# A fused attention and two-layer MLP kernel: where the word between three integer steps lies (SBUF or PSUM)

## The chip, the cores and the metric

The kernel runs on one core of a Trainium2 chip. The metric is the device time of one execution in microseconds (us), the median of three runs. Engine names in profile rows: PE is TensorE's matmuls, PEld its weight loads, DVE is VectorE, ACT is ScalarE, POOL is GpSimd, SP is SyncE (which issues the DMAs here).

## The reference

Masked attention over 4 batches, 8 heads, 576 positions and 64 values per head (heads 0 to 3 see the last 32 positions, heads 4 to 7 every 32nd one), then two layers of an MLP on 2304 tokens of width 512, each with a hidden width of 2048:

```
attn = softmax(mask(q @ k.T / 8)) @ v            # float32
x = attn as (2304, 512)
h = maximum(x @ w_in, 0);  x = (h * h) @ w_out               # first layer
h = x @ w_in2;  g = P(h) / Q(h);  out = g @ w_out2           # second layer
```

P is a cubic and Q a quadratic polynomial in h (Q with absolute values). The weights of both layers reach the kernel as 64-bit floats, which it turns into 32-bit ones itself.

## The kernel before, in words

**Work.** Tokens lie in 6 blocks j of 384. For a block and each of 16 hidden slices f, an "h unit" (line 406, 12 matmuls) gives h[j, f] in a PSUM bank, `act1` (lines 411 to 421) squares its positive part and splits it into a rounded part gh and a remainder gl, and an "acc unit" (line 433, 12 matmuls) adds gh and gl times the second weights into four PSUM banks. In block 0 `act1` works in place: relu (L411), square (L412) and the rounding cast to gh (L420) on ScalarE, the subtraction to gl (L421) on VectorE. The second layer does the same with P/Q in place of the square.

**Weights.** Slice f of the first layer comes in two parts (part 0 for h, part 1 for acc), so there are 32 conversions, called here the 1st to the 32nd, in the order 0_0, 1_0, 2_0, 0_1, 3_0, 1_1, 4_0, 2_1, 5_0, 3_1, ... 15_0, 13_1, 14_1, 15_1 (slice_part). Each is: a DMA of the raw 64-bit words (`load_w`, L185, 512 KB, ring `wraw` of 3 buffers), then `to_f32`: one ScalarE activation (L195) writes a scaled absolute value into a word of the ring `w32` (3 buffers), and three VectorE integer steps (L196, L197, L198) finish the word; L197 and L198 also read the raw words. Then `split_w` makes the rounded weights wh (GpSimd L214, every fourth time ScalarE L212) and the remainder wl (GpSimd L215, the first four on VectorE). The DMA of conversion n+3 waits for L198 of conversion n.

**Attention.** 48 groups of a head pair go through slots: scores (L271 mask, L279), maximum (L290), exponential (L303), normalization (L311, L312, L314), transposes (L321), values (L337), output (L362, L363). Groups 0 to about 11 come first; the next run between the units of block 0.

**PSUM.** All PSUM tiles (ps_s, ps_t, ps_v, h, the four acc) are taken from one pool of 8 banks under one tag (`bufs=8`). A tile that takes a bank waits until the tile that had it is done with.

**Order.** A list scheduler in the framework orders each engine's instructions from the program's order, dependences and free buffers; at run time each engine takes its own list strictly in order. In the first layer the order of the conversions among other work is the scheduler's. The second layer's conversions (the same `to_f32`, with layer 1) run during blocks 1 to 4 and go back to DRAM.

Of the kernel before, what the change touches and what calls it, by code (L numbers as in the profile page):

```python
# [11 lines left out]
I32 = mybir.dt.int32  # L12
BF16 = mybir.dt.bfloat16
AF = mybir.ActivationFunctionType
ALU = mybir.AluOpType
# [3 lines left out]
P = 128  # L19
# [3 lines left out]
DM, DFF = 512, 2048  # L23
# [133 lines left out]
def moe_kernel(ctx, tc, qk, vp, w1, w2, a, b, masks, eye, out):  # L157
    nc = tc.nc
# [14 lines left out]
    psum = ctx.enter_context(tc.tile_pool(name="psum", bufs=8, space=PSUM))  # L173
# [14 lines left out]
    def to_f32(layer, f, part, raw):  # L188

        lo, hi = raw[:, :, 0], raw[:, :, 1]
        w = stage.tile([P, DM], I32, tag="w32", bufs=3, name=f"w32_{layer}_{f}_{part}")
        wf = w.bitcast(F32)
        nc.scalar.activation(wf, hi.bitcast(F32), AF.Abs, scale=2.0**-112)  # L195
        nc.vector.tensor_scalar(w, w, 3, 0x7FFFFFFF, ALU.logical_shift_left, ALU.bitwise_and)  # L196
        nc.vector.scalar_tensor_tensor(w, hi, -0x80000000, w, ALU.bitwise_and, ALU.bitwise_or)  # L197
        nc.vector.scalar_tensor_tensor(w, lo, 29, w, ALU.logical_shift_right, ALU.bitwise_or)  # L198
        return wf

    def w_place(layer, f):
# [263 lines left out]
    def feed_w(n):  # L465
        for _ in range(n):
            if wq:
                f, part = wq.pop(0)
                c = slice(part * DM, (part + 1) * DM)
                wh, wl = wt[0, f] if part else w_place(0, f)  # L470
                split_w(wh[:, c], wl[:, c], to_f32(0, f, part, load_w(0, f, part)))
# [14 lines left out]
    def spill_w(f, part):  # L486

        wf = to_f32(1, f, part, load_w(1, f, part))
        parts = [stage.tile([P, DM], F32R, tag="w32", bufs=3, name=f"sp{c}{f}_{part}") for c in "hl"]
        split_w(*parts, wf)  # L490
        for z, t in enumerate(parts):
            nc.sync.dma_start(w2_dram[z, f][:, part * DM : (part + 1) * DM], t.bitcast(F32))
# [97 lines left out]
    for j, f in steps:  # L590
# [10 lines left out]
        ps = psum.tile([P, 512], F32, tag="ps", name=f"h0_{j}_{f}")  # L601
# [46 lines left out]
```

## Time and profile before

| | |
|---|---|
| time of three runs | 951.86 us median (951.51 to 952.64) |
| the profiled execution | 951.99 us, of which the span of the profile is 950.2 us |
| busy, share of the span | PE 95%, DVE 73%, POOL 64%, ACT 58% |
| 60 to 95 us | PE 28.0 of 35 us, DVE 33.4, POOL 27.6 |
| 95 to 130 us | PE 27.6 of 35 us, DVE 32.8, POOL 28.2 |
| 165 to 240 us | PE 74.4 of 75 us, DVE 40.9 |
| 570 to 950 us | PE 375.6 of 380 us, DVE 373.4 |

The span is the time between the first and the last recorded instruction. Busy times of engines overlap. PEclk in the rows is the share of TensorE's full clock that was granted. A wait of an engine is put down to the instruction that released it.

### The profile page before, as it was taken

The page shows a single profiled execution, that of the slowest core. Times are in us where ns is not written, and L with a number is a line of the kernel's source. Part 1 is how long each engine was busy: PE and PEld are TensorE (multiplying, and loading weights), DVE is VectorE, ACT ScalarE, POOL GpSimd, SP SyncE. Part 2 cuts the span into 40 slices and gives each one's busy share as a digit, 9 for nine tenths or more (in the row PEclk, how much of TensorE's full clock was granted, in tenths as well). Part 3 has the DMA queues.
Part 4 walks back from the last instruction along what each step waited for, and adds up shares of the span by engine and source line. Part 5 has one row for each costly group of instructions (what it writes and reads, how often), then busy time and mean ns, then how long its engine had stood idle before and what let it go on. Part 6 is the DMA issues. An engine that isn't in the chain of part 4 may idle for free.

```text
span 950.2 us, 14600 instructions
## 1 busy us (share of the span) xinstructions
PE 903.5 (95%) x5232; PEld 830.8 (87%) x5232; DVE 691.4 (73%) x792; ACT 548.8 (58%) x1391; POOL 609.6 (64%) x643
## 2 busy tenths in 40 slices
PE   7787689999999999999999999999999999999998
PEld 4576679999899989999999999999999899899896
DVE  3789993554545555544411579999999999999997
ACT  4765454453544445433323667676777777777774
POOL 3667772545545545534423468888888888888885
PEclk9798888999999999999999999999999999999999
DMA  8256451543533463434158550010010010000000
GB/s 306 82 177 206 142 184 67 180 159 121 191 128 107 147 196 101 133 133 134 67 203 285 187 175 18 9 51 9 9 50 9 9 51 10 15 28 1 34 1 34
DMA packets 40104, 98.55 MB, mean 104 GB/s; under 512 B 4704, under 2 KB 11616, under 8 KB 40032
## 3 DMA queue, kind: packets, MB, share of 16 engines
q1 hardware_dynamic: 40032, 97.62, 31.0%
q8 instruction: 41, 0.67, 0.3%
q14 instruction: 31, 0.25, 0.1%
HBM read 71.39 MB, written 26.21 MB: 103 GB/s over the span
## 4 chain that ended last, share of the span: by engine, by line
DVE 46%; PE 39%; POOL 5%; ACT 4%; issue 3%; DMA 2%; SPq 0%; POOLq 0%; ACTq 0%; DVEq 0%
DVE rq L530 23%; PE h L406 19%; PE acc L433 16%; DVE p L532 9%; DVE rq L541 7%; DVE w L197 2%; DVE w L198 2%; POOL wl L215 1%; PE ps_t L321 1%; DVE w L196 1%; PE ps_s L279 1%; PE ps_v L337 1%; DMA qk<-in_qk 1%; POOL wh L214 1%; DMA x_scratch<-x 1%
## 5 line engine op out<-in xcount | busy, mean ns | idle before, releaser
L406 PE MATMUL h<-xh,wh 128*128 128x384 f32 x768 | 259.5, 338 | 0.6 <-ACT p L527 0.5
L406 PE MATMUL h<-xh,wl 128*128 128x384 f32 x768 | 258.3, 336 | 0.0
L406 PE MATMUL h<-xl,wh 128*128 128x384 f32 x768 | 257.8, 336 | 0.0
L530 DVE RECIPROCAL rq<-w 128x384 f32<-128x384 f32 x96 | 243.9, 2541 | 17.2 <-POOL w L528 17.2
L406 PEld LDWEIGHTS h<-xh,wh 128*128 128x128 f32 x768 | 144.8, 189 | 6.8 <-ACT p L527 1.9
L406 PEld LDWEIGHTS h<-xl,wh 128*128 128x128 f32 x768 | 144.8, 188 | 3.8
L421 POOL TENSOR_TENSOR gl<-r,gh 128x384 fp32r<-128x384 f32 x75 | 75.8, 1011 | 110.2 <-ACT gh L420 96.1
L406 PEld LDWEIGHTS h<-xh,wl 128*128 128x128 f32 x768 | 144.5, 188 | 0.0
L549 POOL TENSOR_TENSOR gl<-rq,gh 128x384 fp32r<-128x384 f32 x96 | 115.1, 1199 | 39.8 <-ACT gh L548 39.8
L433 PE MATMUL acc<-gh,wh 128*128 128x384 f32 x384 | 132.6, 346 | 2.0 <-ACT gh L420 2.0
L433 PE MATMUL acc<-gl,wh 128*128 128x384 f32 x384 | 132.1, 344 | 2.0 <-DVE gl L421 2.0
L417 DVE TENSOR_TENSOR r<-r 128x384 f32<-128x384 f32 x75 | 57.1, 761 | 103.6 <-ACT r L416 103.3
L433 PE MATMUL acc<-gh,wl 128*128 128x384 f32 x384 | 131.4, 342 | 0.0
L528 POOL TENSOR_TENSOR w<-w,sq 128x384 f32<-128x384 f32 x96 | 97.4, 1014 | 46.6 <-ACT sq L525 46.6
L529 POOL TENSOR_TENSOR p<-p,hs 128x384 f32<-128x384 f32 x96 | 114.6, 1194 | 0.0
L563 PE MATMUL acc<-wh,gl 128*128 128x512 f32 x288 | 114.1, 396 | 0.2 <-POOL gl L549 0.2
L563 PE MATMUL acc<-wl,gh 128*128 128x512 f32 x288 | 113.7, 395 | 0.0
L563 PE MATMUL acc<-wh,gh 128*128 128x512 f32 x288 | 112.0, 389 | 0.0
L548 ACT CAST gh<-rq 128x384 fp32r<-128x384 f32 x96 | 49.4, 514 | 105.9 <-DVE rq L541 105.9
L532 DVE SCALAR_TENSOR_TENSOR p<-p,co,hs 128x384 f32<-128x384 f32 x96 | 99.2, 1033 | 0.0
L416 ACT ACTIVATE r<-h 128x384 f32<-128x384 f32 x75 | 36.7, 490 | 87.9 <-PE h L406 83.6
L420 ACT CAST gh<-r 128x384 fp32r<-128x384 f32 x75 | 38.5, 514 | 72.0 <-DVE r L417 71.8
(71 smaller groups left out, 1627.2 us busy)
## 6 DMA issues: line engine op xcount, KB each, us to landing
wraw<-in_w SPq DMA_DIRECT2D x64, 512.0 KB, 4.2
w_scratch<-sph SPq DMA_DIRECT2D x32, 256.0 KB, 4.1
w_scratch<-spl SPq DMA_DIRECT2D x32, 256.0 KB, 3.3
wh<-w_scratch SPq DMA_DIRECT2D x16, 512.0 KB, 3.7
wl<-w_scratch SPq DMA_DIRECT2D x16, 512.0 KB, 4.8
v<-in_vp SPq DMA_DIRECT2D x24, 256.0 KB, 4.6
qk<-in_qk SPq DMA_DIRECT2D x12, 416.0 KB, 5.0
x_scratch<-x SPq DMA_DIRECT2D x24, 192.0 KB, 2.6
```

The source lines that it names most:

```text
L406: nc.tensor.matmul(ps[:, :TB], w[:, c], x[:, kk, :], start=(kk == 0 and i == 0), stop=(kk == KT - 1 and i == 2))
L417: nc.vector.tensor_tensor(h, h, h, ALU.mult)
L421: (nc.vector if psum_h else nc.gpsimd).tensor_tensor(gl, h, gh.bitcast(F32), ALU.subtract)
L433: nc.tensor.matmul(acc[j][e][:, :TB], w[:, c], g, start=(f == 0 and i == 0), stop=(f == NF - 1 and i == 2))
L528: keep(nc.gpsimd.tensor_tensor(w, w, sq, ALU.add))
L529: keep(nc.gpsimd.tensor_tensor(p1, p1, hs, ALU.mult))
L530: keep(nc.vector.reciprocal(rq, w))
L532: keep(nc.vector.scalar_tensor_tensor(p1, p1, a1, hs, ALU.add, ALU.mult))
L541: keep(nc.vector.scalar_tensor_tensor(rq, p1, a0, rq, ALU.add, ALU.mult))
L548: keep(nc.scalar.copy(gh, rq))
L549: keep(nc.gpsimd.tensor_tensor(gl, rq, gh.bitcast(F32), ALU.subtract))
L563: nc.tensor.matmul(p, g[:, t * P : (t + 1) * P], w[:, c], start=(f == 0 and i == 0), stop=(f == NF - 1 and i == 2))
```

## The change

In the first layer alone, the word that goes from the first to the second and from the second to the third integer step is a new tile `bits` of the PSUM pool, in place of the `w32` word itself. The third step writes its result to the `w32` word as before. Nothing is added or taken away: each conversion still has one activation and three VectorE steps of 128x512 words.

```
         nc.scalar.activation(wf, hi.bitcast(F32), AF.Abs, scale=2.0**-112)
-        nc.vector.tensor_scalar(w, w, 3, 0x7FFFFFFF, ALU.logical_shift_left, ALU.bitwise_and)
-        nc.vector.scalar_tensor_tensor(w, hi, -0x80000000, w, ALU.bitwise_and, ALU.bitwise_or)
-        nc.vector.scalar_tensor_tensor(w, lo, 29, w, ALU.logical_shift_right, ALU.bitwise_or)
+        bits = w
+        if layer == 0:
+            bits = psum.tile([P, DM], I32, tag="ps", name=f"bits{f}_{part}")
+        nc.vector.tensor_scalar(bits, w, 3, 0x7FFFFFFF, ALU.logical_shift_left, ALU.bitwise_and)
+        nc.vector.scalar_tensor_tensor(bits, hi, -0x80000000, bits, ALU.bitwise_and, ALU.bitwise_or)
+        nc.vector.scalar_tensor_tensor(w, lo, 29, bits, ALU.logical_shift_right, ALU.bitwise_or)
         return wf
```

The 32 new tiles take their turn in the 8 banks, and the scheduler orders all five engines' lists anew, from the attention slots ahead of block 0 to its h unit 13. Behind that point the lists are the same. (Lines from 196 on move by 3 in the changed file: its integer steps are L199, L200 and L201, its h units L409, its acc units L436.) Three places:

On VectorE, at the last two conversions (14_1 and 15_1), the list before reads:

```order
L421 TENSOR_TENSOR gl_0_12_1469<-h_0_12_1453,gh_0_12_1468 128x384 [waits PE_49,Activation_49]
L198 SCALAR_TENSOR_TENSOR w_0_14_1_1247<-wraw_14_1_1245,w_0_14_1_1247 128x512 [waits DVE_49]
L196 TENSOR_SCALAR w_0_15_1_1256<-w_0_15_1_1256 128x512 [waits Activation_49]
L197 SCALAR_TENSOR_TENSOR w_0_15_1_1256<-wraw_15_1_1254,w_0_15_1_1256 128x512 [waits DMAHW3_49,DVE_49]
L290 TENSOR_REDUCE sm_0_2_1496<-ps_s_0_2_1484 96x4 [waits PE_49]
L198 SCALAR_TENSOR_TENSOR w_0_15_1_1256<-wraw_15_1_1254,w_0_15_1_1256 128x512 [waits DVE_49]
```

and the list of the change:

```order
L424 TENSOR_TENSOR gl_0_7_1250<-h_0_7_1234,gh_0_7_1249 128x384 [waits Activation_49]
L201 SCALAR_TENSOR_TENSOR w_0_13_1_1267<-wraw_13_1_1265,bits_1_1269 128x512 [waits DVE_49,Pool_49]
L199 TENSOR_SCALAR bits_1_1279<-w_0_14_1_1277 128x512 [waits Activation_49]
L200 SCALAR_TENSOR_TENSOR bits_1_1279<-wraw_14_1_1275,bits_1_1279 128x512 [waits DMAHW0_49,DVE_49]
L201 SCALAR_TENSOR_TENSOR w_0_14_1_1277<-wraw_14_1_1275,bits_1_1279 128x512 [waits DVE_49,Pool_49]
L199 TENSOR_SCALAR bits_1_1289<-w_0_15_1_1287 128x512 [waits Activation_49]
L200 SCALAR_TENSOR_TENSOR bits_1_1289<-wraw_15_1_1285,bits_1_1289 128x512 [waits DMAHW1_49,DVE_49]
L201 SCALAR_TENSOR_TENSOR w_0_15_1_1287<-wraw_15_1_1285,bits_1_1289 128x512 [waits DVE_49,Pool_49]
L424 TENSOR_TENSOR gl_0_8_1311<-h_0_8_1295,gh_0_8_1310 128x384 [waits PE_49,Activation_49]
L424 TENSOR_TENSOR gl_0_9_1342<-h_0_9_1326,gh_0_9_1341 128x384 [waits PE_49,Activation_49]
```

Before, the remainders gl of 13 units (0 to 12) stand ahead of the last conversion's third step; now those of 8 units do, and units 8 and 9 come behind it.

On TensorE, at the scores of groups 0_1 and 1_1 (behind h unit 9 in both), the list before has these rows:

```order
L271 MATMUL ps_s_0_1_1325<-cst 96x512
L271 LDWEIGHTS cst
L271 MATMUL ps_s_1_1_1326<-cst 96x512
L279 MATMUL ps_s_0_1_1325<-qk_0_1_837 96x128 [waits DMAHW2_49]
...
L321 MATMUL ps_t_0_0_1343<-ident,e_0_0_1075 128x96 [waits DVE_49]
```

and the list of the change:

```order
L274 LDWEIGHTS cst [waits DVE_49]
L274 MATMUL ps_s_0_1_1357<-cst 96x512 [waits PE_49]
L274 LDWEIGHTS cst
L274 MATMUL ps_s_1_1_1358<-cst 96x512 [waits DVE_49]
L282 MATMUL ps_s_0_1_1357<-qk_0_1_851 96x128 [waits DMAHW7_49]
...
L324 MATMUL ps_t_0_0_1375<-ident,e_0_0_1098 128x96 [waits DVE_49,Pool_49]
```

The tiles of these scores now take the banks of the words of conversions 14_1 and 15_1, and their first matmuls wait for VectorE; ps_t of group 0_0 takes the bank of h unit 9 and waits for gl of unit 9.

On ScalarE, at unit f = 2 of block 0, the list before reads:

```order
L411 ACTIVATE h_0_2_769<-h_0_2_769 128x384 [waits PE_49]
L420 CAST gh_0_1_736<-h_0_1_721 128x384 [waits Activation_49]
L412 ACTIVATE h_0_2_769<-h_0_2_769 128x384 [waits Activation_49]
L420 CAST gh_0_2_784<-h_0_2_769 128x384 [waits Activation_49]
L212 CAST wh_2_464<-w_0_2_1_664 128x512 [waits DVE_49]
```

and the list of the change:

```order
L195 ACTIVATE w_0_8_0_884<-wraw_8_0_882 128x512 [waits DMAHW4_49,Pool_49]
L414 ACTIVATE h_0_2_783<-h_0_2_783 128x384 [waits PE_49]
L415 ACTIVATE h_0_2_783<-h_0_2_783 128x384 [waits Activation_49]
L195 ACTIVATE w_0_6_1_894<-wraw_6_1_892 128x512 [waits DMAHW5_49,DVE_49,Pool_49]
L423 CAST gh_0_2_798<-h_0_2_783 128x384 [waits Activation_49]
```

The cast to gh of unit 2 stood ahead of the activation of conversion 5_0 (the 9th); now it stands behind that of 6_1 (the 16th), which waits for its raw words.

## Rows read from the trace of the kernel before

**Rows 1.** The page: busy time of the engines, and the chain that ended last.
```profile
PE 903.5 (95%) x5232; PEld 830.8 (87%) x5232; DVE 691.4 (73%) x792; ACT 548.8 (58%) x1391; POOL 609.6 (64%) x643
...
DVE 46%; PE 39%; POOL 5%; ACT 4%; issue 3%; DMA 2%; SPq 0%; POOLq 0%; ACTq 0%; DVEq 0%
```

**Rows 2.** Windows: stretch, length, busy PE, PEld, DVE, ACT, POOL, clock, DMA, GB/s.
```profile
60.00:95.00 35.00, 28.03 (x175) 25.18 (x176) 33.40 (x51) 19.20 (x59) 27.61 (x29) 0.90 0.65 208
95.00:130.00 35.00, 27.63 (x160) 25.64 (x159) 32.80 (x44) 17.75 (x48) 28.15 (x28) 0.85 0.51 171
...
165.00:240.00 75.00, 74.43 (x518) 70.83 (x517) 40.89 (x69) 35.73 (x110) 39.05 (x49) 1.00 0.49 156
```

**Rows 3.** Timeline of VectorE, 60 to 150 us: start, duration, instruction, [idle before].
```profile
61.82 0.68 DVE L198 SCALAR_TENSOR_TENSOR w<-wraw,w 128x512 int32<-128x512 int32 x1
...
96.81 0.17 DVE L312 RECIPROCAL sm<-sm 96x4 f32<-96x4 f32 x1 [2.46 <-POOL sm L311]
...
113.49 0.41 DVE L196 TENSOR_SCALAR w<-w 128x512 int32<-128x512 int32 x1
113.82 0.55 DVE L421 TENSOR_TENSOR gl<-h,gh 128x384 fp32r<-128x384 f32 x1
114.29 0.68 DVE L197 SCALAR_TENSOR_TENSOR w<-wraw,w 128x512 int32<-128x512 int32 x1
115.00 1.65 DVE L198 SCALAR_TENSOR_TENSOR w<-wraw,w 128x512 int32<-128x512 int32 x1
...
133.88 0.69 DVE L198 SCALAR_TENSOR_TENSOR w<-wraw,w 128x512 int32<-128x512 int32 x1
...
142.60 1.14 DVE L198 SCALAR_TENSOR_TENSOR w<-wraw,w 128x512 int32<-128x512 int32 x1
```

**Rows 4.** Windows of lines 196, 197, 198 alone: length, busy VectorE (count), clock.
```profile
48.00:149.00 101.00, 19.86 (x27) 0.87 0.56 181
...
48.00:149.00 101.00, 24.70 (x28) 0.87 0.56 181
...
48.00:149.00 101.00, 34.36 (x28) 0.87 0.56 181
```

**Rows 5.** Groups by line and shape, 0 to 240 us: busy, mean ns, idle before.
```profile
L417 DVE TENSOR_TENSOR r<-r 128x384 f32<-128x384 f32 x16 | 12.6, 787 | 13.3 <-ACT r L416 13.3
...
L290 DVE TENSOR_REDUCE sm<-ps_s 96x4 f32<-96x512 f32 x16 | 10.7, 677 | 0.0
...
L421 DVE TENSOR_TENSOR gl<-h,gh 128x384 fp32r<-128x384 f32 x16 | 8.8, 549 | 8.9 <-ACT gh L420 8.8
...
L288 DVE TENSOR_TENSOR ps_s<-ps_s,cst 96x512 f32<-96x512 f32 x4 | 2.6, 688 | 1.8 <-PE ps_s L279 1.8
```

**Rows 6.** DMA issues, 60 to 130 us: count, KB each, median us to landing.
```profile
wraw<-in_w SPq DMA_DIRECT2D x20, 512.0 KB, 3.9
```

**Rows 7.** Timeline of ScalarE, around 51 and 106 to 117 us.
```profile
51.52 1.30 ACT L195 ACTIVATE w<-wraw 128x512 f32<-128x512 f32 x2
...
106.47 0.48 ACT L420 CAST gh<-h 128x384 fp32r<-128x384 f32 x1
...
116.69 0.62 ACT L212 CAST wh<-w 128x512 fp32r<-128x512 f32 x1 [1.24 <-DVE w L198]
```

**Rows 8.** The chain of waits from 145 us: start, duration, what.
```profile
147.01 3.49 PE h L406 x12
...
159.17 2.08 PE h L406 x12
161.25 2.08 PE acc L433 x12
```

**Rows 9.** Timeline of TensorE: scores at 107, values and transposes at 135 to 139 us.
```profile
107.72 0.60 PE L271 MATMUL ps_s<-cst 96*96 96x512 bf16 x2
108.25 1.12 PE L279 MATMUL ps_s<-qk 64*96 64x128 f32 x16
...
135.43 0.55 PE L337 MATMUL ps_v<-at,v 128*64 128x96 f32 x8 [0.40 <-DVE gl L421]
...
139.19 0.52 PE L321 MATMUL ps_t<-ident,e 96*128 96x96 f32 x4 [3.21 <-POOL wh L214]
```

## The prediction

> **What bounds the kernel now.** The page comes first: TensorE is busy 95% of the span, yet VectorE holds 46% of the chain that ended last and TensorE 39% [rows 1]. Both can only be true if different stretches have different limits, so the windows come next [rows 2]. [...] From 165 to 240 us TensorE works 74.43 of 75 us. So first-layer conversions are VectorE's stretch, and what is gained or lost there passes to the end one for one: behind it TensorE is dense, and its instructions there are the same in both kernels.
>
> Then the conversions themselves. The 8th ends at 61.82 + 0.68 = 62.50 us, the 32nd at 142.60 + 1.14 = 143.74 us [rows 3]: 81.24 us for 24, or 3.39 each. One step is not one price: the third step took 0.69 us at 133.88 and 1.65 us at 115.00 [rows 3]. Grouped by line, the three steps cost 19.86, 24.70 and 34.36 us between 48 and 149 us, for 27, 28 and 28 instructions [rows 4]: 78.9 us, 2.82 per conversion. The reason to look for is in the neighbours: a subtraction of 128x384 with both inputs in SBUF (L417) took 787 ns, the one with one input in PSUM (L421) 549 ns [rows 5], while GpSimd was busy about 28 of 35 us throughout [rows 2].
>
> **The change part by part.** *The steps.* The trace has no integer step on PSUM. Bounds: an elementwise operation from and to PSUM, 512 wide, took 688 ns, a reduce of 512 from PSUM 677 ns, L421 549 ns for 384, which is 0.73 for 512 by width [rows 5]. Below, the first step could keep its present 0.41 [rows 3] and the others 0.68; above, nothing is shortened and each keeps today's means, 0.74, 0.88 and 1.23 [rows 4]. I take 0.69 for each, by the L288 row, which is nearest: 2.07 per conversion. Then 28 conversions cost 58.0 in place of 78.9 us, 21 us less of VectorE's time (the first step alone gets dearer, by 0.28 on an undisturbed one). There are no new instructions and no new DMAs.
>
> The rows show no dearer price for PSUM: 688 and 677 ns there, 0.68 and 0.69 us for undisturbed steps in SBUF [rows 3, 5]. [...]
>
> *Can the conversions use it?* A ring of three raw words feeds them: landing 3.9 us [rows 6], the activation 1.30 / 2 = 0.65 [rows 7], three steps 2.07, handoffs 0.2 (chosen), together 6.82 for three conversions, 2.27 each. VectorE's own pace is 2.07 plus 8 subtractions gl of 0.55 over 24 conversions, 2.25. So about 2.3 us per conversion is what both allow, against 3.39 now. If all was as before and nothing else waited, 24 x 1.09 = 26 us would be free, more than TensorE could use: it was idle only about 7 of each 35 us [rows 2].
>
> *The order.* The banks change more than the steps. The new words take turns with scores, transposes, values, h and acc, and the scheduler puts conversions far ahead: only units 0 to 7 have their gl before the last conversion ends, before it was 0 to 12. TensorE's work is no less; more of it lies behind the last conversion. What that costs is counted from the end of the 32nd conversion to the start of h unit 13.
>
> Before: 147.01 - 143.74 = 3.27 us [rows 3, 8], and unit 13 itself ran at the low clock, 3.49 in place of 2.08 us [rows 8], another 1.41. Together 4.68.
>
> Now: ScalarE first casts wh (0.62 [rows 7]) and does five operations of units 8 and 9 of 0.48 each [rows 7], VectorE the gl of 0.55 [rows 5], handoffs 0.2, together 3.8, before the transposes of group 0_0 can go on, since they take the bank that this gl releases. Then TensorE has three h units (3 x 2.08 = 6.24), acc 8, 9, 10 and 7 of the 12 matmuls of acc 11 (3.58 x 2.08 = 7.45) [rows 8], one pair of scores (from 107.72 to 109.37, 1.65), three value products (0.55 for two, 0.83) and four transposes (4 x 0.52 = 2.1) [rows 9]. That is 18.2, with the 3.8 before it 22.0. The work is the same that was done earlier; before, it lay beside conversions in TensorE's idle time.
>
> So the break-even is a 32nd conversion that ends at 143.74 + 4.68 - 22.0 = 126.4 us. By the pace alone it ends well ahead of that; the question is how many waits come on top.
>
> *When does the 32nd end?* The 8th: four of the first eight lie in the stretch of [rows 4], 4 x 0.75 = 3.0 us less; and the activation at 51.52 [rows 7], which the new order puts ahead of attention work, gives 2 more (an estimate): 57.5. Then 24 x 2.3 = 55.2. Attention on VectorE between them: four reduces (two of 0.68, two on fewer scores, taken at half), four reciprocals of 0.17 and eight narrow subtractions taken at the same 0.17 [rows 3, 5]: 4.1. Then the waits that the new order makes:
> - gl of unit 2 follows the 14th conversion, but its cast gh now stands on ScalarE behind the activation of the 16th, whose DMA starts only when the 13th is done. 3.9 + 0.65 + 0.48 + 0.2 after the 13th, 2.3 of it covered by the 14th: 2.9 us in which the conversions queued behind it wait.
> - Reciprocals stand close behind their reduces. One such wait for GpSimd was 2.46 [rows 3]; taken once more, 2.5.
> - Three conversions whose activation stands behind another unit's three ScalarE operations (3 x 0.48): 4.2.
> - h units 3 and 5 whose acc follows directly leave TensorE idle, and the next unit then runs at the low clock, 1.4 us more each by [rows 8]: 2.8.
>
> That is 12.4, and the end 57.5 + 55.2 + 4.1 + 12.4 = 129.2 us, 2.8 behind the break-even. The profiled execution lasted 951.99 us, 0.13 above the median of 951.86, which lies on its span of 950.2 with 1.8 outside. 951.99 + 2.8 = 954.8.
>
> **The rivals.** *Faster: the waits are short.* The same chain, with the other sign. If the DMAs run ahead (landing 3.9 is a median) and the reciprocals' waits lie under other steps, only 5 or 6 us of the 12.4 remain, the 32nd ends near 122.8, and h unit 13 starts 3.6 us earlier: 948.4. For it: 21 us off the engine that is the bound is much, and only 2.8 us in 129 lie between the two; against it: VectorE's list is strictly in order, and each of its new waits holds all conversions. It decides when the end falls below 126.4.
>
> *No change.* Gain and tail cancel to within 1.9 us, an end between 124.5 and 128.3: about 952.
>
> *The low clock.* TensorE had 0.85 to 0.90 in this stretch [rows 2] and goes through a unit in 3.49 at the low clock. If, with acc waiting behind each h, the clock falls for six units in place of two, 4 x 1.41 = 5.6 us are added: about 960.
>
> *The change does not do what it says.* The steps stay as long as today, because GpSimd is not what stretches them or because the raw word in SBUF is enough for it. Then 24 conversions take 24 x 2.82 = 67.7 in place of 55.2, and the tail stays: about 967.
>
> **How the numbers follow.** The forecast of a late 32nd conversion with a long tail has 0.48; its own range, with 0.1 us either way per conversion, is 952.4 to 957.2. The short waits have 0.27, no change 0.11, the low clock 0.11, unshortened steps 0.03. A difference under 0.2% (1.9 us) can't be told from no change here; of the forecast's 0.48, 0.10 falls under it, of the short waits 0.02. Faster 0.25, same 0.10 + 0.11 + 0.02 = 0.23, slower 0.38 + 0.11 + 0.03 = 0.52. The range takes in the faster case and the low clock (960.4), 947 to 961, and leaves out the last rival and the ends of the others.
>
> **What would show it.** In the changed profile each of the three lines should have a mean near 0.69 with none above 0.8 in block 0, and their sum should be near 58 us for 28 conversions; means near 0.88 and 1.23 would mean that the change does nothing. The 32nd third step should end near 129 us; below 124 the waits were overestimated. TensorE's idle time should lie before that end, and from there to h unit 13 it should be dense for about 18 us, with unit 13 starting near 151 at 2.08 us. Stretches behind that should be as before; a difference there would be outside this sum. VectorE should show idle time ahead of gl of unit 2 and of two reciprocals. If conversions come at 2.3 us and the end is still not moved, the tail is the step that is right; if TensorE idles in the tail, the order costs more than I counted.

## The result, and the profile after

The change takes 964.98 us (median of four runs, 963.24 to 968.75) against 952.15 us: a ratio of 1.0140, 95% interval 1.0109 to 1.0171, or 12.8 us slower. The profiled execution took 963.24 us, the shortest of the four, with a span of 961.1 us, 10.9 us longer than that of before. The direction was forecast, the size was not: 954.8 us, with a range to 961.

The page of the change gives busy times and, further down, the chain that ended last; VectorE is busy 19 us less than before [rows 1], and the span grew:

```profile
PE 904.0 (94%) x5232; PEld 830.9 (86%) x5232; DVE 672.1 (70%) x792; ACT 551.6 (57%) x1391; POOL 593.9 (62%) x643
...
DVE 44%; PE 42%; ACT 4%; DMA 4%; POOL 3%; issue 2%; SPq 0%; ACTq 0%; POOLq 0%; DVEq 0%
```

The groups of VectorE by line and shape, 0 to 240 us, show the steps; each has 32 instructions, and their means stand in ns:

```profile
L200 DVE SCALAR_TENSOR_TENSOR bits<-wraw,bits 128x512 int32<-128x512 int32 x32 | 21.9, 690 | 0.8 <-DVE sm L315 0.3
L199 DVE TENSOR_SCALAR bits<-w 128x512 int32<-128x512 int32 x32 | 21.8, 689 | 7.4 <-ACT w L195 7.2
L201 DVE SCALAR_TENSOR_TENSOR w<-wraw,bits 128x512 int32<-128x512 int32 x32 | 21.7, 682 | 1.9 <-DVE bits L200 0.5
```

The windows of the change, with the stretches of [rows 2] first, then 48 to 149 us and the 24 conversions from the end of the 8th (58.34 + 0.69 = 59.03 us) to the end of the 32nd (135.87 + 0.69 = 136.56 us):

```profile
60.00:95.00 35.00, 20.31 (x110) 17.60 (x111) 23.85 (x44) 16.74 (x41) 20.01 (x26) 0.80 0.52 173
95.00:130.00 35.00, 23.39 (x115) 20.71 (x114) 25.40 (x45) 17.15 (x46) 22.99 (x26) 0.80 0.61 197
165.00:240.00 75.00, 74.43 (x498) 71.81 (x497) 37.00 (x63) 34.38 (x103) 35.77 (x45) 1.00 0.40 126
...
48.00:149.00 101.00, 69.65 (x393) 61.75 (x394) 67.66 (x125) 52.93 (x148) 59.14 (x74) 0.85 0.53 175
...
59.03:136.56 77.53, 49.70 (x258) 43.74 (x257) 54.37 (x97) 37.18 (x91) 47.72 (x56) 0.82 0.55 182
```

VectorE went from 33.4 to 23.9 of 35 us busy, and TensorE with it, from 28.0 to 20.3. Nobody is full in this stretch any more: the bound is a chain that passes through several engines and the DMAs in turn. Behind it TensorE is as dense as before.

What VectorE waited for in those 24 conversions (total, times, longest), and the largest wait of ScalarE from 48 to 149 us:

```profile
DVE gl L424 <- ACT gh L423: 9.1, 3, 4.2
DVE bits L199 <- ACT w L195: 7.2, 7, 1.7
DVE sm L315 <- POOL sm L314: 2.5, 2, 1.4
DVE xl L366 <- ACT xh L365: 1.9, 3, 0.9
...
ACT w L195 <- DMA wraw<-in_w: 23.3, 16, 3.4
```

The timeline of VectorE, third steps of the 8th and the 32nd conversion:

```profile
58.34 0.69 DVE L201 SCALAR_TENSOR_TENSOR w<-wraw,bits 128x512 int32<-128x512 int32 x1
...
135.87 0.69 DVE L201 SCALAR_TENSOR_TENSOR w<-wraw,bits 128x512 int32<-128x512 int32 x1
```

One turn of that chain, from the chain of waits (start, duration, what), and the row of it at which h unit 13 starts (159.15):

```profile
68.38 0.70 DVE w L201
69.08 0.02 SPq L185
69.10 0.04 issue
69.14 3.85 DMA wraw<-in_w
...
73.07 0.46 ACT w L195
73.53 4.39 DMA wraw<-in_w
...
78.03 0.66 ACT w L195
78.69 0.38 ACT gh L423
79.07 0.02 issue
79.09 0.57 DVE gl L424
79.66 0.14 issue
79.80 1.07 PE ps_t L324 x4
...
159.15 2.08 PE h L409 x12
```

Read it from the top: a third step ends and frees a raw word; the DMA lands; the activation on it runs. The next DMA starts at 73.53, when the third step of the 13th conversion has freed its word; it lands, the activation of the 16th runs, and only then comes the cast gh, which stood in ScalarE's list behind it; then gl, and TensorE goes on. The squares of unit 2 that gh casts were done by 74.62 us (74.15 and 0.47 on ScalarE). TensorE's timeline says what the wait was worth there:

```profile
79.80 1.07 PE L324 MATMUL ps_t<-ident,e 126*126 126x126 f32 x4 [3.76 <-DVE gl L424]
```

The same form comes again at unit 6, where TensorE's acc waits for the cast, and not VectorE's gl. What VectorE then waits for at unit 7 is a cast that only follows its own late h unit (ScalarE, TensorE and VectorE, in order of time):

```profile
121.99 0.66 ACT L195 ACTIVATE w<-wraw 128x512 f32<-128x512 f32 x1 [2.05 <-DMA wraw<-in_w]
122.56 0.46 ACT L423 CAST gh<-h 128x384 fp32r<-128x384 f32 x1
123.07 1.65 PE L436 MATMUL acc<-gh,wh 128*128 128x384 f32 x4 [4.87 <-ACT gh L423]
...
129.63 0.47 ACT L414 ACTIVATE h<-h 128x384 f32<-128x384 f32 x1 [2.75 <-PE h L409]
131.15 0.56 DVE L424 TENSOR_TENSOR gl<-h,gh 128x384 fp32r<-128x384 f32 x1 [2.79 <-ACT gh L423]
```

### The profile page after: what moved, and what is told of

It is laid out like the page before. It is cut to its first block, busy times and chain, and to the rows that moved or that the text cites. A ratio compares the mean times of both kernels' runs of the same rounds, so it can differ in the third digit from the quotient of the medians.

```text
span 961.1 us, 14616 instructions
## 1 busy us (share of the span) xinstructions
PE 904.0 (94%) x5232; PEld 830.9 (86%) x5232; DVE 672.1 (70%) x792; ACT 551.6 (57%) x1391; POOL 593.9 (62%) x643
## 4 chain that ended last, share of the span: by engine, by line
DVE 44%; PE 42%; ACT 4%; DMA 4%; POOL 3%; issue 2%; SPq 0%; ACTq 0%; POOLq 0%; DVEq 0%
DVE rq L533 23%; PE h L409 20%; PE acc L436 17%; DVE p L535 9%; DVE rq L544 7%; DMA wraw<-in_w 3%; PE ps_t L324 1%; PE ps_s L282 1%; PE ps_v L340 1%; DVE w L201 1%; ACT w L195 1%; DMA qk<-in_qk 1%; DVE r L420 1%; DMA x_scratch<-x 1%; ACT e L306 1%
## 5 line engine op out<-in xcount | busy, mean ns | idle before, releaser
L409 PE MATMUL h<-xh,wh 128*128 128x384 f32 x768 | 261.0, 340 | 6.7 <-ACT h L415 3.1
L409 PE MATMUL h<-xh,wl 128*128 128x384 f32 x768 | 259.7, 338 | 0.0
L409 PE MATMUL h<-xl,wh 128*128 128x384 f32 x768 | 259.4, 338 | 0.0
L409 PEld LDWEIGHTS h<-xh,wh 128*128 128x128 f32 x768 | 145.8, 190 | 13.0 <-ACT h L415 3.4
L409 PEld LDWEIGHTS h<-xl,wh 128*128 128x128 f32 x768 | 145.9, 190 | 3.8
L409 PEld LDWEIGHTS h<-xh,wl 128*128 128x128 f32 x768 | 145.8, 190 | 0.0
L436 PE MATMUL acc<-gh,wh 128*128 128x384 f32 x384 | 130.2, 344 | 14.2 <-ACT gh L423 9.8
L436 PE MATMUL acc<-gl,wh 128*128 128x384 f32 x384 | 131.3, 342 | 0.0
L436 PE MATMUL acc<-gh,wl 128*128 128x384 f32 x384 | 130.4, 340 | 0.0
L436 PEld LDWEIGHTS acc<-gh,wh 128*128 128x128 f32 x384 | 72.7, 190 | 16.5 <-ACT gh L423 9.6
```

Source lines behind the costliest of these rows:

```text
L409: nc.tensor.matmul(ps[:, :TB], w[:, c], x[:, kk, :], start=(kk == 0 and i == 0), stop=(kk == KT - 1 and i == 2))
L436: nc.tensor.matmul(acc[j][e][:, :TB], w[:, c], g, start=(f == 0 and i == 0), stop=(f == NF - 1 and i == 2))
```

## The experiments

Theory A: the order and the bank waits cost the time. Theory B: the shorter steps run into the ring of three raw words whatever the order. Each run stands beside runs of the kernel before on the same chip (medians 952.1 to 953.1 us); "ahead of gl 9" is the number of conversions that VectorE's list has ahead of the gl of unit 9: 23 before, 32 in the change. (Added lines of code move the lines in a run's rows, by one in the fourth and seven in the sixteenth run.)

**Bank held, words in SBUF.**

```
+            bits = psum.tile([P, DM], I32, tag="ps", name=f"bits{f}_{part}")
+            nc.vector.memset(bits[:, :2], 0)
         nc.vector.tensor_scalar(w, w, 3, 0x7FFFFFFF, ALU.logical_shift_left, ALU.bitwise_and)
...
+            nc.vector.memset(bits[:, :2], 0)
```

> Words in SBUF as in the kernel before, but each conversion also holds a PSUM bank: a tile of the common pool whose first two columns VectorE sets to zero ahead of the first and behind the third step (64 more tiny VectorE operations; the output stays the same). The list then has the front-loaded order of the change. Theory A, the order that the banks make is what costs: the long steps come back on top of it, so it is as slow as the change or slower, 964 to 976 us. Theory B, the shorter steps run into the ring of three raw words, whatever the order: with the long steps and their pace as before, about 952 to 957 us.

Measured: 969.32 us (ratio 1.0170, 1.0153 to 1.0187; 31 ahead of gl 9). The order and the bank waits cost some 16 us with long steps, of which the 64 zeroings of 60 ns are up to 4. Short steps on top of it (the change) gave back only 4.3 us. Theory A held, and theory B's 952 to 957 us is out.

**Two conversions offered per unit**, with the words in PSUM and, as control, in SBUF: `feed_w(2)` for `feed_w(3)`.

> The change, and two conversions offered to the scheduler per unit of block 0 in place of three, which puts the gl of unit 9 ahead of the 25th conversion, nearly as before. Theory A: the shorter steps then count and the tail is short, so the 32nd conversion ends near 130 us with little work behind it, 936 to 945 us. Theory B: the ring holds the pace above 3 us per conversion, 950 to 960 us.

> The control: the kernel before with two conversions offered per unit in place of three; its order changes little. Both theories: 949 to 956 us, with steps as long as before (0.74, 0.88 and 1.23 us on average in the stretch of the conversions).

Measured: 951.89 us (0.9968 to 0.9999; 25 ahead of gl 9) and 953.95 us (0.9998 to 1.0022). Taking the front-loading away is worth 13 us, but the step gain of some 10 us that I expected on top did not come: VectorE still waited 13.7 us for gh. The time lies in theory B's range, not in theory A's, and the 24 conversions took 149.66 - 60.52 = 89.1 us, 3.7 each: this run by itself does not speak for theory A.

**One bank of its own for the word**, seven for the rest.

```
-    psum = ctx.enter_context(tc.tile_pool(name="psum", bufs=8, space=PSUM))
+    psum = ctx.enter_context(tc.tile_pool(name="psum", bufs=7, space=PSUM))
+    bpool = ctx.enter_context(tc.tile_pool(name="bpool", bufs=1, space=PSUM))
...
+            bits = bpool.tile([P, DM], I32, tag="bits", name=f"bits{f}_{part}")
```

> The change, but the word between the steps has one bank of its own and the other tiles share seven. The list then has the conversions no earlier than the kernel before (6 ahead of the first gl, 20 ahead of that of unit 9). Theory A: 936 to 948 us. Theory B: 950 to 960 us. If seven banks in place of eight cost much by themselves, it is above 952 with short steps.

> The own bank of the fourth run with the words in SBUF, the bank only held (VectorE zeroes two of its columns ahead of the first and behind the third step; the output stays the same). The order is about that of the kernel before. Theory A (the order and the banks decide, and the short steps count only where VectorE does not wait): long steps bind VectorE again, 950 to 960 us, so that the short steps are worth 8 to 16 us here, against 4 us with the common pool. Theory C, the own bank by itself is the gain: about 943 us, as with short steps.

> The kernel before with seven banks in place of eight and nothing else. Theory A: 949 to 956 us. Theory C, the other order of a pool of seven is the gain: about 943 us.

Measured: 942.64 us (0.9852 to 0.9914) with the word in PSUM, 963.43 us (1.0066 to 1.0146) with the bank only held, 965.89 us (1.0107 to 1.0174) with seven banks and nothing else. Theory C is out, and seven banks alone cost 14 us, more than I expected; the zeroings of the fifth run cost nothing that shows beside it. Here the short steps are worth 963.43 - 942.64 = 20.8 us, in the common pool 969.32 - 964.98 = 4.3 us. The windows of 48 to 149 us (TensorE's busy time comes first, VectorE's third) show where: words in SBUF with the common pool, then with the own bank, then the own bank with words in PSUM:

```profile
48.00:149.00 101.00, 70.01 (x367) 61.15 (x364) 91.66 (x182) 49.86 (x140) 67.59 (x74) 0.77 0.53 171
```

```profile
48.00:149.00 101.00, 78.22 (x473) 68.67 (x471) 89.80 (x139) 57.81 (x171) 76.68 (x78) 0.90 0.55 181
```

```profile
48.00:149.00 101.00, 92.53 (x600) 84.07 (x599) 78.67 (x147) 64.52 (x186) 65.92 (x84) 0.97 0.60 196
```

With its own bank, TensorE goes from 78 to 93 us busy when the steps get short; in the common pool it stays at 70 (70.01 and, in the change, 69.65). The two lists with the own bank are close, not equal: 20 conversions stand ahead of gl 9 with short steps, 24 with long ones.

The chain of waits shows where the own bank wins and where it loses: the rows that begin with h unit 13 of block 0, short steps and then long ones.

```profile
125.87 4.16 PE h L410 x24
```

```profile
149.35 4.18 PE h L412 x24
```

Before, the unit starts at 147.01 [rows 8], and from there to the end of the span it is 950.2 - 147.01 = 803.2 us; in the fourth run it is 940.7 - 125.87 = 814.8. So short steps with a bank of their own win 21 us by h unit 13, and behind it, with seven banks for the rest, nearly 12 are lost again.

**Casts first.** The step's conversions are issued behind the unit's activation on ScalarE (`with tc.issue_after(last_act): feed_w(3)`).

> The change, with the conversions of a unit's step issued behind that unit's activation on ScalarE, so that no cast gh stands behind an activation that waits for raw words of a later step; units 0 to 9 then have their gl ahead of the last conversion, before 0 to 7. Theory A1, those casts are what VectorE and TensorE waited for: the waits of gl for gh (10.7 us in the change) and of acc for gh (9.8) mostly go, 948 to 957 us. Theory A2, the front-loading costs what it costs by TensorE's work behind the last conversion: 960 us or more.

Measured: 972.71 us (1.0183 to 1.0248). Theory A1 fell: gl still waits 12.6 us for gh. No cast stands behind a later step's activation any more, but VectorE now waits 9.0 us for the activations, and the list is still front-loaded (32 ahead of gl 9).

**Two banks for the words**, six for the rest.

> Two banks for the words between the steps and six for the rest; the conversions stand further ahead than with one bank (25 ahead of the gl of unit 7, 19 in the kernel before, 29 in the change). Theory A: between the two, 945 to 956 us. If it is only that the words share no bank with others: as with one bank, about 943.

Measured: 1005.83 us (1.0532 to 1.0601), outside both expectations. From 240 to 570 us, where no word of the first layer is converted, TensorE is busy 302.6 us, 324.2 before: six banks are too few for the later blocks, and this run tells nothing of the words.

**TensorE's lag.** The h and acc matmuls of block 0 kept in the program's order.

> The change, with TensorE's h and acc matmuls of block 0 kept in the program's order, so that acc of a unit comes two units behind its h in place of directly behind it. VectorE's list is the one of the change, front-loaded (gl of units 0 to 7 ahead of the last conversion). Theory L, the ping-pong of h, cast, gl and acc of one unit is what made the waits that were mis-sized: TensorE's 9.8 us for gh go, VectorE's 10.7 us for gh mostly too, 952 to 960 us. Theory F, the front-loaded list is the cost whatever TensorE's lag is: 961 to 968 us, with the waits of VectorE for gh still there.

> The second run (two conversions offered per unit, words in the common pool) with the same lag of two units on TensorE. Theory L: its waits for gh (13.7 us on VectorE, 10.5 on TensorE) mostly go, 940 to 948 us. Theory F: this order is not front-loaded, so nothing is left to gain by the lag, 949 to 955 us.

> The control: the kernel before with TensorE's block 0 kept in the program's order, which changes it at a few places, for it had the lag of two units at most of them. Both theories: 949 to 956 us.

Measured: 969.64 us (1.0142 to 1.0182), 953.95 us (1.0002 to 1.0029) and 952.21 us (0.9983 to 1.0009). Theory L fell, though the ninth run is slower than theory F had it, too. In it acc no longer waits for gh, but h units wait 11.7 us for third steps to free their banks or weights: the wait only changed its place.

**The eighth bank given back** behind block 0, to every third h unit (`bpool.tile(...) if j and f % 3 == 0`), in both layers.

> The fourth run (one bank of its own for the word, seven for the rest), with that bank given to every third h unit behind block 0, so that eight banks are in use again there. The lists of block 0 are those of the fourth run. Where that run lost to the missing bank, TensorE's idle time from 240 to 570 us (9.5 against 5.8 us in the kernel before), some 3 to 5 us should come back: 936 to 941 us. If one bank in rotation of its own makes these units wait: 943 us or more.

Measured: 942.36 us (0.9867 to 0.9897), no better than the fourth run.

**Conversions offered later.** `if slot > 14: feed_w(1)` (for 9) and `feed_w(2)`; the fourteenth run has 12.

> The change with its conversions offered later: none during the slots ahead of block 0 and two per unit in block 0. The words stay in the common pool of eight banks, but the list now has the conversions where the run with one bank of its own had them (20 ahead of the gl of unit 9, 18 ahead of that of unit 8). Theory O, the place of the conversions in the list decides: about as with the own bank, 938 to 946 us, and VectorE's waits for gh below 5 us. Theory S, sharing banks with scores, values and h units costs by itself: 949 to 956 us, with those waits as in the second run (13.7 us).

> Between the second and the thirteenth run: 22 conversions ahead of the gl of unit 9 (25 and 20 there, 32 in the change). Theory O: between the two, 943 to 950 us. Theory S: 949 to 956 us.

> The control: the late offer with the words in SBUF (the kernel before, 21 conversions ahead of the gl of unit 9 as there). Both theories: VectorE is bound by the long steps and nothing is gained, 950 to 960 us.

Measured: 950.05 us (0.9961 to 0.9995), 950.79 us (0.9951 to 0.9989) and 952.02 us (0.9979 to 1.0005). The thirteenth run has, to within two, as many conversions ahead of each gl from unit 3 to unit 11 as the fourth, and is still 7 us slower, with all that seven banks cost that one. The ranges favour theory S. But the late offer also starts the conversions late: the 8th ends at 75.5 us, in the fourth run at 59.55, and h unit 13 starts at 141.74 us, in the fourth run at 125.87, so the two runs are some 16 us apart at both ends of the stretch. With long steps the late start costs nothing (fifteenth run); with short steps it was not tested by itself, so sharing banks is not shown to be the cause. The waits of VectorE from 48 to 149 us, first here, then in the fourth run:

```profile
DVE gl L424 <- ACT gh L423: 11.3, 10, 3.7
```

```profile
DVE gl L425 <- ACT gh L424: 2.0, 7, 0.5
```

**The loads left out.** Every conversion of the first layer reads one of the first three raw words again.

```
+        if layer == 0 and len(kept) >= 3:
+            kept.append(kept[-3])
+            return kept[-1]
```

> The change with the loads of the first layer's raw words left out, but for the first three: every later conversion reads one of these three again, so its numbers are not the weights', and no activation waits for a landing. The list stays front-loaded as in the change (28 conversions ahead of the gl of unit 7, 29 ahead of that of unit 8). Theory R, the waits come from the chain third step, DMA landing, activation, cast behind it, gl: they go, the 32nd conversion ends at 118 to 124 us, and by the break-even of 126.4 us the time is 944 to 950 us. If the waits stay without the loads (ping-pong by the banks): 960 us or more.

> The same left out of the kernel before. The scheduler then front-loads here too (28 conversions ahead of the gl of unit 7, in the kernel before 20). Long steps bind VectorE whether words land or not, and the tail is as long as in the change: 960 to 972 us under both theories.

Measured: 957.78 us (1.0035 to 1.0065) and 964.24 us (1.0101 to 1.0139). Without landings the change gets 7.2 us back, with the 32nd conversion at 129.10 in place of 136.56 us, and not the 15 to 21 that theory R expected. The kernel before gets slower by 11.7 us without them, since its list is then front-loaded too (31 ahead of gl 9); beside it, short steps are worth 964.24 - 957.78 = 6.5 us. So even with no landing to wait for, a front-loaded list in the common pool gives little of the steps' 21 us. In the sixteenth run gl waits 20.1 us for gh from 48 to 149 us, 12.4 in the change. What ScalarE waits for now is the next ring, the words w32, whose buffers GpSimd's remainders free (the view of waits, total, times, longest):

```profile
ACT w L202 <- POOL wl L225: 26.6, 23, 3.1
```

**The own bank, given back in the first layer alone.**

> The twelfth run, with the eighth bank given back in the first layer alone (every third h unit of blocks 1 to 5), and the second layer in seven banks as in the fourth run, where it lost nothing. The twelfth run ended the first layer's h units at 514.9 us against 522.1 in the fourth and 532.0 before, and lost 7 us of it in the second layer. If that comes through: 933 to 938 us. If the second layer gives it back anyway: 940 to 944 us.

Measured: 937.27 us (0.9813 to 0.9846), 15.3 us faster than the kernel before and the fastest of all. The eighth bank in rotation of its own helps the first layer, and only there: given to the second layer as well (twelfth run), the gain is gone.

## Why the prediction missed

*The steps: right.* 0.69 was taken, 0.689, 0.690 and 0.682 measured, with none stretched. The second and third, which read PSUM, took 0.690 and 0.682, where unstretched third steps that read SBUF took 0.68 and 0.69 [rows 3]: no dearer price for PSUM shows here either. The rival of unshortened steps is out.

*The tail: right.* From the 32nd conversion to h unit 13 I counted 22.0 us; it is 159.15 - 136.56 = 22.6, with TensorE dense.

*The break-even: right.* The 32nd conversion ended 136.56 - 126.4 = 10.2 us behind it, and the span grew by 10.9.

*The waits that the new order makes, 12.4 us: wrong, and this is the step that failed.* The 8th conversion ended at 59.03 (57.5 forecast), the next 24 took 77.53 us (71.7 forecast). Of these VectorE was busy 54.37 and idle 23.16. By my working the pace and the attention needed 59.3 and the waits 12.4; the work was 4.9 us less than I allowed and the waits 10.8 us more. Item by item:

- First steps behind their activations: 7.2 against 4.2 (3 x 1.44 is 4.3), and for another reason. I priced three activations behind another unit's operations on ScalarE. One of the seven waits is of that kind (1.69 us, at 91.59). In five of them, 5.4 us together, the activation had itself waited for its raw words: the ring of three, which I took to deliver every 2.3 us with its landings covered, did not. ScalarE waited 23.3 us for landings between 48 and 149 us, 12.3 before, and beyond that pace I had put a price on it at unit 2 alone.
- gl behind its cast: 9.1 in three waits against 2.9 in one. At unit 2, as priced, the cast stood behind the activation of the 16th conversion, and the wait was 4.2: the landing took 4.4 us in place of 3.9, and the 14th conversion covered 1.4 of it in place of 2.3. At units 5 and 7 (2.1 and 2.8) no activation stood between: the cast followed an h unit that TensorE ran late, after its acc had waited 3.96 us for the cast of unit 4 and 4.87 for that of unit 6. At unit 6 the cast stood behind an activation that waited for its landing, the form that I had priced for unit 2; at unit 4 the relu did (activation at 97.99, its wait 2.40).
- The reciprocals: 2.5, as forecast. The output's subtractions: 1.9, which I had not counted. The 2.8 for h units 3 and 5 have no row of their own among VectorE's waits. The rest is many small gaps.

So I found the mechanism at one place of VectorE's list, and did not look for its copies in the waits of TensorE, which come back to VectorE one unit later.

*The low clock* was granted at 0.80 in both stretches (0.90 and 0.85 before [rows 2]), but the rival's step is not there: it wanted six units slowed in place of two, and in the trace 42 matmuls of h and acc took over 0.46 us between the 8th conversion and 175 us, where before 45 did up to 165 us. Part of the low grant fell on time in which TensorE waited (0.50 from 76.0 to 79.8 us, where TensorE was busy 0.04 us); in the own-bank run, with the same steps, the clock is 0.97 over 48 to 149 us. The faster rival and no change are out.

*Where the 21 us went.* From 60 to 130 us VectorE's busy time fell by 17 us, from 33.40 + 32.80 [rows 2] to 23.85 + 25.40, and turned into waits. Shown: two conversions offered per unit in place of three take 13 us back (the change against the second run); the landings are worth 7.2 us (sixteenth run); and the same steps are worth 20.8 us where the word has a bank of its own (fourth against fifth run), by h unit 13 already. That this is so near to the 21 us that I had worked out is in part luck, as the two lists are not equal. Out as causes: the lag of acc, and the order of the casts alone. Open stays how much of what is left between the common pool and the own bank comes from the shared banks' waits and how much from the order and the start of the conversions; the rings of raw words and of w32 words only argue for a chain through several engines, in which taking one link out uncovers the next. A list of the own bank with the common pool's banks was not tried.

## What to carry to other kernels

A scratch tile that goes into the pool of the accumulators also goes into the scheduler's plan: look first at what the new list puts where, and try the scratch in a bank of its own; here that paid even at the price of one bank for the rest (942.64 us, 964.98 in the common pool). A saving on a busy engine need not shorten the span: here, with a list that had become a chain with loads and casts, 17 us less busy time of VectorE from 60 to 130 us turned into waits, and the span grew by 10.9 us. A wait found at one place of a list should be counted at every place of the same form, and on every engine that waits there, before it goes into a sum.

## What the runs showed of the hardware

- VectorE's steps and GpSimd's operations were long together and got short together: with the words in PSUM, the three steps went from 0.74, 0.88 and 1.23 us [rows 4] to 0.689, 0.690 and 0.682, GpSimd's remainders from 1523 to 1279 ns and its rounding from 777 to 621 ns on average, 48 to 149 us, though nothing of GpSimd was changed. With the own bank it is the same: with the words in SBUF (fifth run) the steps took 0.74, 0.93 and 1.02 us on average and GpSimd was busy 76.68 us for 78 instructions in that stretch, with the words in PSUM (fourth) 0.687, 0.688 and 0.681 us and 65.92 us for 84. The rows are those of the change and of before:

```profile
L218 POOL TENSOR_TENSOR wl<-w,wh 128x512 fp32r<-128x512 f32 x28 | 35.8, 1279 | 10.9 <-ACT wh L215 9.0
L217 POOL TENSOR_SCALAR wh<-w 128x512 fp32r<-128x512 f32 x21 | 13.0, 621 | 11.4 <-DVE w L201 11.1
```

```profile
L215 POOL TENSOR_TENSOR wl<-w,wh 128x512 fp32r<-128x512 f32 x28 | 42.6, 1523 | 9.8 <-ACT wh L212 8.3
L214 POOL TENSOR_SCALAR wh<-w 128x512 fp32r<-128x512 f32 x21 | 16.3, 777 | 8.3 <-DVE w L198 7.9
```

- The first step, one input and a scalar, took 0.41 us from SBUF to SBUF at 113.49 us [rows 3] and 0.689 on average with its output in PSUM (0.677 at the shortest).
- Where one wait was taken out, another of its size came up: 11.7 us of TensorE for third steps in place of 9.8 us for casts (ninth run), 26.6 us of ScalarE for GpSimd's remainders in place of 23.3 us for landings (sixteenth run).
